# TensorE takes its work in a written-out order, and P is transposed by a product with identity columns, out of one pool of seven PSUM banks

## The chip, the core and the metric

The kernel runs on one core of a Trainium2 chip. Five engines matter: TensorE multiplies matrices and writes its results to PSUM (PE in the profile, with its weight loads as PEld), VectorE (DVE) and ScalarE (ACT) compute and copy, GpSimd (POOL) does small things, and SyncE (SP) issues DMAs. PSUM is taken by the kernel as eight banks of 128 partitions by 512 f32. The metric is device microseconds of one execution; less is better. The kernel before took 2958.28 us, the median of three runs (2955.21 to 2960.57).

## The reference

The input x has 2048 tokens of 576 numbers. Two layers follow one another, and each is a recurrent attention and a gated feed-forward part, with the same weights in both layers:

```python
x = x + _A_ref(_layernorm(x), mem0, Wq, Wk, Wv, Wo, 32)
x = x + _B_ref(_layernorm(x), w1, w3, w2)      # twice in all

def _A_ref(x, mem0, ...):                      # 32 heads of 128; 8 memory rows; 64 segments of 32 tokens
    for s in range(64):
        h = concatenate([mem, x[segment s]])   # 40 rows
        q, k, v = h @ Wq, h @ Wk, h @ Wv
        p = softmax(where(mask, q k^T * scale, -1e9))
        o = (p v) @ Wo
        mem = o[:8]                            # the next segment needs it
        outs.append(o[8:])

def _B_ref(x, ...):
    return (silu(x @ w1) * (x @ w3)) @ w2      # 4608 hidden numbers
```

The memory rows make the segments of one layer a chain: segment s+1 of a layer can't begin its products before the output product of segment s is through.

## The kernel before, in words

**Steps.** The work goes in 72 steps. Step t does segment t of the first layer and segment t - 8 of the second (`LAG` is 8). Steps 0 to 7 have the first layer alone and steps 64 to 71 the second alone, with 40 columns (32 tokens and 8 memory rows); steps 8 to 63 have both side by side, 80 columns, in the same instructions. The heads of a step go in four groups g of eight.

**Units of TensorE work.** `make_nodes` makes a list of nodes; each TensorE node is a run of matmuls that is never split. By one letter each, with the number of matmuls: Q (32, products of Wq and Wk with the segment, two per group) and q (8, the last 64 rows of that contraction); S (16, or 8 in a step of one layer: the scores of a group); T (8, the transposition of the softmax's result P of a group); P (16, P times V); O (40, the output product); X and x (32 and 8, V of the tokens), V and v (the same for the memory rows); F (36, the first products of the feed-forward part on one pair of hidden blocks; in the last job 16, with its remainder f as a unit of its own) and W (8, the second product); m, n, p (transpositions around layernorm and residual; 5 each; the list of the change has a, b and n for the three sorts that are all n here).

**Shapes of the array.** The units use the array in five ways, which the nodes carry as `mode`: full (128 rows by 128 columns of array: Q, T, O, W and the transpositions, and the first products F of the last job), row (64 rows: q, P, F, f), col (128 by 64: S), c32 (128 by 32: X, V) and oct (64 by 32: x, v).

**The order.** `plan` walks a model of the engines in time. At each step it takes the engine that can begin first, and for TensorE the waiting node with the best key: its priority, plus `o.wait` for a late start, plus a penalty `o.mode_pen` for a change of shape. The nodes of the other engines are taken by priority alone. A node marked AD goes to ScalarE or VectorE, whichever the model has free first. The list that comes out is emitted as it stands, and `ch` chains the instructions of each engine in that order, so the order is fixed when the kernel is built; on the chip each engine still waits for the data.

**PSUM.** Six banks form the pool `bank`; most units take two of them and give them back when VectorE or ScalarE has read them. The bank `YB` collects O over a step. The bank `SB` is a pool of one, `s`, and is used in turn by S (f32 scores, 320 columns) and T (bf16). The planner chooses the bank numbers.

**The softmax chain of a group.** S writes the scores; VectorE adds the mask, takes the maximum and subtracts it; ScalarE takes the exponential; VectorE sums, inverts and multiplies into the tile `PB`, which has the first layer's rows at 0 to 39 and the second's at 64 to 103, and zeros elsewhere where they matter. T (`ptr`) turns `PB` round with eight transposing matmuls against the first 104 columns of `ident`, and `pt_ev` copies the 40 or 80 wanted columns of each out of `SB` to `PTS` in one instruction. P reads `PTS`, `ot_ev` copies its two banks to `OT`, and O reads `OT`. After the last O of a step, `y_mem` copies the memory rows from `YB` into `HT`, which Q of the next step reads.

**In the profile** all matmuls stand under line L498, ScalarE's work under L501 and VectorE's under L504, so groups are told apart by their tiles: Q and q are `bank<-HT,W`, S is `SB<-QKT`, T is `SB<-ident,PB`, P is `bank<-PTS,VX` and `bank<-PTS,VM`, O is `YB<-OT,WO`, X, x, V, v are `bank<-WV,HT`, F is `bank<-XTB,W` and W is `bank<-W2C,HTT`.

Of the kernel before, what the change touches and what calls it, by code (L numbers as in the profile page):

```python
# [37 lines left out]
POOLS = {"bank": 6, "s": 1, "y": 1, "qkt": 4, "vx": 2, "vm": 1, "sme": 2, "pb0": 1, "pb1": 1, "pts": 1, "ot": 1,  # L38
# [29 lines left out]
def plan(nodes, pools, o):  # L68
# [12 lines left out]
    order = []  # L81

    def push(n):
        (both if n.eng == "AD" else ready[n.eng]).append(n)

    def slots_at(n):
        t = 0.0
# [3 lines left out]
        for p, c in need.items():  # L91
            f = sorted(free[p])
            t = max(t, f[c - 1])
# [5 lines left out]
    done = 0  # L99
    idle = 0.0  # L100
    while done < len(nodes):
        best = None
        for e in t_eng:
            cands = ready[e] + (both if e in ("ACT", "DVE") else [])
            if not cands:
                continue
            ests = [(max(t_eng[e], n.ready, slots_at(n)), n) for n in cands]
# [5 lines left out]
        if best is None:  # L113
            stuck = [(n.name, n.prio) for e in ready for n in ready[e]][:20]
            raise RuntimeError(f"the plan is stuck: {stuck}")
# [11 lines left out]
        st, n = min(pool_, key=key)  # L127
# [3 lines left out]
        if n.eng == "AD":  # L131
            both.remove(n)
        else:
            ready[e].remove(n)
        if e == "PE":
            idle += max(0.0, st - t_eng[e])
            if n.mode != mode:
                dur += SWITCH
                mode = n.mode
        n.start, n.end, n.by = st, st + dur, e  # L140
        t_eng[e] = n.end
        for s in n.acq:
            f = free[s.pool]
            ok = [i for i in range(len(f)) if f[i] <= st + 1e-9]
            s.i = min(ok, key=lambda i: f[i])
# [6 lines left out]
        for o_ in n.outs:  # L152
            lat = n.lat
# [979 lines left out]
```

## Time and profile before

| What | us |
|---|---|
| median of three runs | 2958.28 |
| the profiled execution, its own time | 2961.47 |
| its span, first to last instruction | 2959.4 |
| TensorE busy (matmuls) | 2870.1 |
| VectorE busy | 2060.5 |
| ScalarE busy | 1150.1 |
| TensorE's mean granted clock | 0.985 |

The profile is of one execution, so its own time is what its rows add up to, and the median is 3.2 us below it. A matmul's listed duration (about 200 ns for most) includes its way through the array and overlaps with the next one's; what a matmul costs TensorE is the distance from its start to the start of the next. So the costs are read from the starts of neighbouring rows in the timeline, not from the mean durations.

### The profile page before, as it was taken

What the parts mean: (1) busy time and instruction counts of PE and PEld (TensorE: products, weight loads), DVE (VectorE), ACT (ScalarE), POOL (GpSimd) and SP (SyncE); (2) the same over time, 40 slices, a digit from 0 to 9 for tenths busy, and PEclk for the clock granted to TensorE, in tenths of its full rate; (3) what the DMA queues carried; (4) which work ended last, traced back from release to release, by engine and by line L of the source; (5) the groups of instructions that cost most, each with busy time, mean ns of one, the idle gap of its engine ahead of it and who ended that gap; (6) DMA issues with size and microseconds to landing.
All of it is one profiled execution on the core that took longest, in us unless ns stands there. A gap on an engine that the chain in (4) does not pass through costs nothing.

```text
span 2959.4 us, 146757 instructions
## 1 busy us (share of the span) xinstructions
PE 2870.1 (97%) x67733; PEld 2328.3 (79%) x67733; DVE 2060.5 (70%) x4939; ACT 1150.1 (39%) x2759; POOL 63.6 (2%) x108
## 2 busy tenths in 40 slices
PE   5899999999999999999999999999999999999987
PEld 4777878788888878887887887888788888887876
DVE  3566676776777677676777777677767767776765
ACT  1334443343434343343434334343433434343332
POOL 0000000000000000000000000000000000000000
PEclk8899999999999999999999999999999999999998
DMA  9055544434443433444343443434344344434567
GB/s 299 4 117 125 114 106 109 109 88 108 99 99 93 109 101 93 105 100 106 91 100 96 109 100 90 115 91 107 89 109 108 87 109 97 99 94 114 125 152 221
DMA packets 483561, 324.43 MB, mean 110 GB/s; under 512 B 16888, under 2 KB 478080, under 8 KB 482944
## 3 DMA queue, kind: packets, MB, share of 16 engines
q1 hardware_dynamic: 479872, 307.96, 42.9%
q8 instruction: 529, 8.67, 1.3%
q0 software_dynamic: 3072, 7.08, 0.8%
q14 instruction: 88, 0.72, 0.1%
HBM read 310.26 MB, written 2.36 MB: 106 GB/s over the span
## 4 chain that ended last, share of the span: by engine, by line
PE 91%; DMA 3%; issue 2%; DVE 2%; ACT 1%; SPq 1%; POOL 0%; POOLq 0%; DVEq 0%; ACTq 0%
PE bank L498 71%; PE YB L498 12%; PE SB L498 7%; DMA W<-in_B_w_dram 1%; DMA W<-in_A_Wk_dram 1%; ACT HT L501 1%; SPq L507 1%; DVE SME L504 0%; DVE STAT L504 0%; DVE HTT L504 0%; DVE PB L504 0%; DMA W2C<-in_B_w_dram 0%; DVE XR L504 0%; DVE LNS L504 0%; ACT XTB L501 0%
## 5 line engine op out<-in xcount | busy, mean ns | idle before, releaser
L498 PEld LDWEIGHTS <-W 128*128 128x128 bf16 (+1 forms) x34256 | 1229.3, 97 | 138.0 <-issue 43.0
L498 PE MATMUL bank<-HT,W 128*128 128x80 bf16 (+2 forms) x23040 | 815.4, 197 | 8.9 <-issue 2.5
L498 PE MATMUL bank<-XTB,W 64*128 64x256 bf16 (+2 forms) x11216 | 619.6, 260 | 15.4 <-DMA W<-in_B_w_dram 9.7
L498 PE MATMUL bank<-WV,HT 128*32 128x512 bf16 (+3 forms) x8000 | 468.6, 387 | 12.2 <-DMA WV<-in_A_Wv_dram 5.7
L498 PE MATMUL YB<-OT,WO 128*128 128x80 bf16 (+1 forms) x11520 | 437.1, 198 | 8.9 <-ACT OT L501 2.9
L501 ACT ACTIVATE QKT<-bank 128x320 bf16<-128x320 f32 (+1 forms) x694 | 249.8, 405 | 487.4 <-PE bank L498 485.4
L498 PEld LDWEIGHTS <-WO 128*128 128x128 bf16 x11560 | 413.8, 99 | 30.2 <-issue 22.5
L498 PEld LDWEIGHTS <-HT 128*32 128x32 bf16 (+3 forms) x8000 | 174.4, 93 | 237.3 <-issue 99.2
L504 DVE TENSOR_REDUCE STAT<-SME 104x8 f32<-104x320 f32 (+1 forms) x576 | 277.2, 481 | 93.3 <-ACT SME L501 86.9
L504 DVE SCALAR_TENSOR_TENSOR HTT<-HTT,bank 128x512 bf16<-128x512 bf16 (+1 forms) x324 | 200.6, 619 | 202.1 <-ACT HTT L501 199.7
L504 DVE TENSOR_TENSOR PB<-SME,STAT 40x256 bf16<-40x256 f32 (+1 forms) x1024 | 320.9, 318 | 17.9
L504 DVE CAST QKT<-bank 128x320 bf16<-128x320 f32 (+1 forms) x458 | 198.7, 453 | 170.7 <-PE bank L498 170.2
L498 PE MATMUL bank<-W2C,HTT 128*128 128x288 bf16 x2232 | 315.2, 287 | 0.5
L501 ACT ACTIVATE HTT<-bank 128x512 bf16<-128x512 f32 (+1 forms) x324 | 177.7, 548 | 324.4 <-PE bank L498 323.1
L504 DVE SCALAR_TENSOR_TENSOR XR<-bank,XR 128x288 f32<-128x288 f32 x576 | 248.4, 453 | 75.0 <-PE bank L498 65.0
L498 PEld LDWEIGHTS <-HTT 128*128 128x128 bf16 x2304 | 208.4, 98 | 54.3 <-DVE HTT L504 2.6
L501 ACT ACTIVATE OT<-bank 128x320 bf16<-128x320 f32 (+1 forms) x394 | 149.5, 408 | 240.8 <-PE bank L498 240.2
L501 ACT ACTIVATE PTS<-SB 128x640 bf16<-128x640 bf16 (+1 forms) x250 | 162.2, 649 | 185.8 <-PE SB L498 185.3
L504 DVE TENSOR_TENSOR HTT<-HTT,bank 128x512 bf16<-128x512 bf16 (+1 forms) x324 | 203.6, 628 | 32.0 <-DVE HTT L504 0.5
L501 ACT ACTIVATE SME<-SME 104x320 f32<-104x320 f32 (+1 forms) x288 | 135.6, 471 | 209.8 <-DVE SME L504 209.0
L504 DVE CAST VX<-bank 128x512 bf16<-128x512 f32 x115 | 79.4, 691 | 136.4 <-PE bank L498 131.8
L504 DVE TENSOR_TENSOR SME<-SB,maskb 104x320 f32<-104x320 f32 (+1 forms) x288 | 140.5, 488 | 46.4 <-PE SB L498 42.0
(64 smaller groups left out, 1863.1 us busy)
## 6 DMA issues: line engine op xcount, KB each, us to landing
W<-in_B_w_dram SPq DMA_DIRECT2D x612, 288.0 KB, 4.7
W2C<-in_B_w_dram SPq DMA_DIRECT2D x306, 288.0 KB, 3.3
W<-in_B_w_dram SPq DMA_DIRECT2D x10, 512.0 KB, 9.8
XR<-in_A_x_dram POOLq DMA_DIRECT2D x16, 288.0 KB, 3.0
WO<-in_A_Wo_dram SPq DMA_DIRECT2D x4, 1152.0 KB, 9.0
W<-in_A_Wq_dram SPq DMA_DIRECT2D x8, 512.0 KB, 8.6
W<-in_A_Wk_dram SPq DMA_DIRECT2D x8, 512.0 KB, 9.7
WV<-in_A_Wv_dram SPq DMA_DIRECT2D x4, 1024.0 KB, 12.5
```

The costliest lines, as they stand in the source:

```text
L498: self.ch("PE", self.nc.tensor.matmul(out, lhsT=lhsT, rhs=rhs, start=start, stop=stop, skip_group_check=True, **k))
L501: self.ch("ACT", self.nc.scalar.activation(*a, **k))
L504: self.ch("DVE", getattr(self.nc.vector, fn_)(*a, **k))
L507: self.ch("SP", self.nc.sync.dma_start(out=out, in_=in_))
```

## The change

There are three edits. **The order:** `plan` takes a string `ORDER` with one letter per TensorE unit, and TensorE's next node is always the next letter's. The string is `FIRST` (707 letters), eleven times `FOUR` (194 letters, four steps), and `LAST` (590 letters); it has as many of each kind as before. ScalarE, VectorE, GpSimd and the DMAs are still placed by the model, by priority. **The transposition:** T becomes an ordinary product. `sel` holds 40 columns of the identity per layer (those at 0 and at 64), and each of T's eight matmuls multiplies `PB` with the 40 or 80 columns in use; the result is f32. T takes two banks of the pool, one for each half, and `pt_ev` becomes two copies, one per bank, each of 160 or 320 f32 columns, and each free to go to ScalarE or VectorE. **The pool:** `SB` is gone, the pool `bank` has seven banks, and S takes one of them.

```diff
-POOLS = {"bank": 6, "s": 1, "y": 1, "qkt": 4, "vx": 2, "vm": 1, "sme": 2, "pb0": 1, "pb1": 1, "pts": 1, "ot": 1,
+POOLS = {"bank": 7, "y": 1, "qkt": 4, "vx": 2, "vm": 1, "sme": 2, "pb0": 1, "pb1": 1, "pts": 1, "ot": 1,
...
+KINDS = {"m0tr": "m", "L0tr": "a", "L1tr": "b", "POST": "p", "Ftr": "n", "QK": "Q", "QKt": "q", "SC": "S", "TR": "T", "PV": "P",
+         "WO": "O", "VX": "X", "VXt": "x", "VM": "V", "VMt": "v", "FF": "F", "FFt": "f", "W2": "W"}
+def plan(nodes, pools, letters):
...
+    kinds = {}
+    for n in nodes:
+        if n.eng == "PE":
+            kinds.setdefault(KINDS[n.name], []).append(n)
+    its = {k: iter(v) for k, v in kinds.items()}
+    seq = [next(its[c]) for c in letters]
+    assert len(seq) == sum(len(v) for v in kinds.values())
...
+            if e == "PE":
+                cands = seq[at:at + 1] if at < len(seq) and seq[at].left == 0 else []
...
-        if e == "PE":
-            pool_ = [x for x in ests if x[0] <= t + o.hor]
-            work = {}
-            for x in pool_:
-                work[x[1].mode] = work.get(x[1].mode, 0.0) + x[1].dur
-            key = lambda x: (x[1].prio + o.wait * (x[0] - t)
-                             + (o.mode_pen - o.bulk * min(work[x[1].mode], 4.0) if x[1].mode != mode else 0.0))
-        else:
-            pool_ = [x for x in ests if x[0] <= t + 1e-9]
-            key = lambda x: x[1].prio
+        st, n = min((x for x in ests if x[0] <= t + 1e-9), key=lambda x: x[1].prio)
...
+FIRST = (
+    "maQQqqXVvxQSQXqQqSTqQPOTqPOSQxqTQqPSOTPXOxQQqqQqSQQqVSqvQTQqqQqPSTOSPOTPTOPaOQQqqQSqXQqQTSxQqqVvSQQqqPSTOPTOPTOP"
+    "OQQqqQQSqVqQSvQqqQTQqPqSXTOSPTOPOTxPXOxQpQqqVSQQqqnvQQSqqFTQQSqPqFOSTFPWTOPFTOPFOXxQQqqQQSqFqQWQSqqFVvSTQQqPqWTO"
+    "PSFOTFPTOWPFOaXxQQqqQQqSVqvQSqFQqWTQSPFqQqTOSPTOWPFTOPFOQQqqFVWQqSQvqFQQSqqFTQPqSWQOTqPSFTOPWTOPObVXxvQQqqpQSXqx"
+    "QnqQQTSqqQPSFqOQTqFPSFOTPFXxOTWPFOVvQqQQqqFSQQqqXxSQqWTQSPqFOTQqFPSTOWPFXTOxPFOWaQQqqQQSqqQVqSXvxQQqFqWTSQPFTOqP"
+    "FSOTFPXWTOxPFOFQQqQqQSqqQqXVvxQqSTSQPqWQOTqPFSOTWPFOTWPObppQXVqxnQqXxQqSQqnQqvQSqQTqFPFSTOQPqWOTSWPFOTXPFFxOWWQQ"
+    "qqQSqVXxvQQqqQSqTQSPqFOTQqFPSWTOFPWTOFPFXxWWOQQqqWSVXxvQaTQqqQQSqFqQQSqqFPWTOFPTWOSWPFXTOWPxXOWQqFxQQqFqSQqVQvSQ"
+    "qqQTWqSQWPqFTOPSTOPFOTWPWObVXxvpXxp"
+)
+FOUR = (
+    "QQqqnQnQSqqQQSqqFTQqFPSQTOqPFSOWTWFPFTOXPxWOWQQqqFSQQqqXVxvSWQTQqqFPSQQTOqqFPWTOaSPFXxOTWPFOWQQqqVvSWQQqqFTQQSqq"
+    "FPXSxOWTQQqqFFPSWTOWPFOTXxPFWOWQQqqVSvQQqqQQTSqqQQqPqSXxOTFPSWTOWPFTOWPWObVXxvppXx"
+)
+LAST = (
+    "QQqqQSnQqqQQqqSnTQPFqFSTOQPqFSOTWWPFXTOPFOxQQqqXxQQSqqWQSWQqqFFVSvTQqPQqTOPSTOFPXOxTWPWOFQQqqWWQQqqFSSQQqqVXxvWT"
+    "QqPSQTqOSFPWTOPFXTOxPWOWQQqFqQQqqFXSxQQSqqFTWQVvqQSqPWOTFPSFOTWWPFOTWPWObVvpQpQqqXxSQQqqnQnSqXxTQQqqQSqFPFTOSPTO"
+    "FPFTOPWOWQQqqVWWvSQQqFqQSqQTqQQqqSPFTOXPSxTOWPFOTFPWOFQqQqFSWWQqQQqFqVvSWTWQqFPFTWOQSqPQOWqFTSFPXWFxTOWPFOWQQqqQ"
+    "SQqqVSvQQqqTQSPqQqTOSPWOTFPTOWPOWpbVXvxnQQqqQQSqFqQQSqqXQTxSqQPqFTOSPWTOFPFTOPWOXxFQQqqQSqFVvQTqFSQWQqqFPSQQFqqO"
+    "TWPSTOPFOTFPXOFxQWQqqQQSqqQqVSFvQTqQPqFSWQqTOSPFTOPFOTWPOQQqqQQSqVvqFQTqSQqPQSqQqWTSOPOTFPTOPOpnWFfFfFfFWFfFfWfF"
+    "fFWfFFWffFfFfWFfFWFffFfWFfFfWW"
+)
+ORDER = FIRST + FOUR * 11 + LAST
...
-            s = Slot("s")
+            s = banks(1)[0]
...
-            pt = Slot("s")
             pts = Slot("pts")
-            tr = node("PE", 8 * 0.046, em.ptr(t, g, pb, pt), deps=[pbs], prio=pf + o.tr, mode="full", acq=[pt, pts], rel=[pb], name="TR")
-            pe_ = node("AD", ewh(8 * c80), em.pt_ev(t, g, pt, pts), deps=[tr], prio=pf, rel=[pt], name="PTe")
+            bt = banks()
+            tr = node("PE", 8 * mm80, em.ptr(t, g, pb, bt), deps=[pbs], prio=pf + o.tr, mode="full", acq=[pts] + bt, rel=[pb], name="TR")
+            pe_ = [node("AD", ew(4 * c80), em.pt_ev(t, g, m, bt[m], pts), deps=[tr], prio=pf, rel=[bt[m]], name="PTe") for m in (0, 1)]
             b = banks()
             ot = Slot("ot")
-            pv = node("PE", 8 * mm80, em.pv(t, g, pts, vx_slots[t, k], b), deps=[pe_] + vme + vx_nodes[t, k], prio=pf + o.pv,
+            pv = node("PE", 8 * mm80, em.pv(t, g, pts, vx_slots[t, k], b), deps=pe_ + vme + vx_nodes[t, k], prio=pf + o.pv,
...
-    def ptr(self, t, g, pb, pt):
-        def f(n):
-            PT = self.T.SB[:].bitcast(BF)[:, 0:GH * 104].rearrange("p (h q) -> p h q", h=GH)
-            for m in (0, 1):
+    def ptr(self, t, g, pb, b):
+
+        def f(n):
+            q0, q1 = self.qcols(t)
+            nq = q1 - q0
+            for m, T in enumerate(self.bk(x) for x in b):
                 for hl in range(4):
-                    self.mm(PT[:, 4 * m + hl, :], self.T.PB[0:104, g % 2, m, 2 * hl:2 * hl + 2, :], self.T.ident[0:104, 0:104],
-                            True, True, is_transpose=True)
-        return f
-
-    def pt_ev(self, t, g, pt, pts):
-        def f(n):
-            ls = self.layers(t)
-            nq = QW * len(ls)
-            b = self.T.SB[:].bitcast(BF)[:, 64 * ls[0]:64 * ls[0] + 1]
-            src = bass.AP(b.tensor, b.offset, [list(b.ap[0]), [104, GH], [64, len(ls)], [1, QW]])
-            dst = self.T.PTS[:, pts.i, 0:GH * nq].rearrange("p (h a q) -> p h a q", h=GH, a=len(ls))
-            self.cp(n, dst, src)
+                    self.mm(T[:, hl * nq:(hl + 1) * nq], self.T.PB[0:104, g % 2, m, 2 * hl:2 * hl + 2, :], self.T.sel[0:104, q0:q1],
+                            True, True)
+        return f
+
+    def pt_ev(self, t, g, m, b, pts):
+        def f(n):
+            q0, q1 = self.qcols(t)
+            w = 4 * (q1 - q0)
+            self.cp(n, self.T.PTS[:, pts.i, m * w:(m + 1) * w], self.bk(b)[:, 0:w])
         return f
...
+    T.sel = sp.tile([P, 2 * QW], BF, name="sel")
-    T.SB = pp.tile([P, 512], F32, name="SB")
+    for li in (0, 1):
+        nc.gpsimd.tensor_copy(T.sel[:, li * QW:(li + 1) * QW], T.ident[:, R64 * li:R64 * li + QW])
-    nc.vector.memset(T.SB[:], 0.0)
-    order, _ = plan(nodes, pools, Opt)
-    for n in order:
+    for n in plan(nodes, pools, ORDER):
```

More of the change, by code (lines that the diff above doesn't have):

```diff
@@ L143, in plan @@
             f = free[s.pool]
-            ok = [i for i in range(len(f)) if f[i] <= st + 1e-9]
-            s.i = min(ok, key=lambda i: f[i])
+            s.i = min((i for i in range(len(f)) if f[i] <= st + 1e-9), key=lambda i: f[i])
             f[s.i] = NOW
@@ L151, in plan @@
                 free[s.pool][s.i] = s.end
-        for o_ in n.outs:
-            lat = n.lat
-            if o_.eng == e == "PE":
-                lat = 0.0
-            o_.ready = max(o_.ready, n.end + lat)
-            o_.left -= 1
-            if o_.left == 0:
-                push(o_)
+        for m in n.outs:
+            m.ready = max(m.ready, n.end + (0.0 if m.eng == e == "PE" else n.lat))
+            m.left -= 1
+            if m.left == 0:
+                push(m)
         order.append(n)
-        done += 1
-    return order, idle
+    return order
 def actc(*ns):
```

41 lines of the change are left out of this document (19 added, 22 removed).

## The prediction

> **What bounds the kernel now.** I read the page first: the engines' totals and the chain that ended last.
>
> ```profile
> span 2959.4 us, 146757 instructions
> PE 2870.1 (97%) x67733; PEld 2328.3 (79%) x67733; DVE 2060.5 (70%) x4939; ACT 1150.1 (39%) x2759; POOL 63.6 (2%) x108
> ...
> PE 91%; DMA 3%; issue 2%; DVE 2%; ACT 1%; SPq 1%; POOL 0%; POOLq 0%; DVEq 0%; ACTq 0%
> ```
>
> TensorE is busy 97% of the span and is 91% of the chain. Since an average hides stages, the next view is the busy time by stretches (first column the stretch, then its length and each engine's busy time, granted clock, DMA share).
>
> ```profile
> core 0: us, PE busy (x) PEld busy (x) DVE busy (x) ACT busy (x) POOL busy (x), PEclk, DMA share, GB/s
> 0.00:278.00 278.00, 229.48 (x6392) 181.10 (x6393) 150.12 (x414) 88.92 (x275) 8.67 (x21) 0.91 0.54 141
> ...
> 448.00:2660.00 2212.00, 2207.40 (x50214) 1788.53 (x50213) 1598.44 (x3752) 889.95 (x2029) 48.35 (x76) 1.00 0.42 100
> 2660.00:2960.00 300.00, 267.97 (x6752) 219.55 (x6750) 191.25 (x467) 95.71 (x274) 3.44 (x6) 0.93 0.61 153
> ```
>
> TensorE's waits in the long middle stretch, all that are listed for it (total us, times, longest):
>
> ```profile
> PE bank L498 <- ACT HT L501: 3.0, 5, 0.6
> ...
> PE bank L498 <- ACT XTB L501: 0.6, 1, 0.6
> ...
> PE bank L498 <- issue: 0.5, 1, 0.5
> ```
>
> In the middle TensorE idles 4.6 us of 2212 (2212.00 - 2207.40): it waits for nothing. So there the time is the sum of what the matmuls cost in TensorE's own line, and only two things can shorten it: cheaper units and cheaper neighbours. Waits are left in the first 278 us (48.5 idle) and the last 300 (32.0 idle).
>
> What a unit costs is read from the starts in the timeline of TensorE (start, length with the pipeline's end, then the group):
>
> ```profile
> 1424.06 0.54 PE L498 MATMUL SB<-ident,PB 104*128 104x104 bf16 x8
> 1424.43 1.60 PE L498 MATMUL YB<-OT,WO 128*128 128x80 bf16 x40
> 1425.96 0.43 PE L498 MATMUL SB<-QKT 128*64 128x40 bf16 x16
> ...
> 1426.72 1.15 PE L498 MATMUL bank<-W2C,HTT 128*128 128x288 bf16 x8
> 1427.71 1.60 PE L498 MATMUL YB<-OT,WO 128*128 128x80 bf16 x40
> 1429.14 0.54 PE L498 MATMUL SB<-ident,PB 104*128 104x104 bf16 x8
> 1429.51 1.15 PE L498 MATMUL bank<-W2C,HTT 128*128 128x288 bf16 x8
> 1430.59 0.21 PE L498 MATMUL bank<-PTS,VX 64*128 64x80 bf16 x2
> ...
> 1436.24 1.60 PE L498 MATMUL YB<-OT,WO 128*128 128x80 bf16 x40
> ```
>
> and, a period later,
>
> ```profile
> 1606.13 1.60 PE L498 MATMUL YB<-OT,WO 128*128 128x80 bf16 x40
> ```
>
> W costs 0.99 when O follows in the same array shape (1426.72 to 1427.71) and 1.08 when P follows in another (1429.51 to 1430.59). O costs 1.43 before T in the same shape (1427.71 to 1429.14) and 1.53 before S (1424.43 to 1425.96). So a change of shape costs 0.09 to 0.10 us, and I take 0.095. The two rows at 1436.24 and 1606.13 are each the last O of a step, four steps apart: a period of the middle is 1606.13 - 1436.24 = 169.9 us.
>
> **Part 1, the order: fewer changes of shape.** Written as letters, the TensorE rows of that period have 194 units and 119 changes of shape. `FOUR` has the same 194 units, so the same matmuls, and by its letters 90 changes (the last letter to the first included). That is 29 fewer in each of eleven periods, 319. Over the whole, from m to the last W, the rows have 2090 changes and the string has 1759; 331 fewer x 0.095 = **31.4 us** less. Nothing hides this, since TensorE waits for nothing there, and nothing is added to it: the same work stands closer.
>
> **Part 2, T with fewer columns.** T is 8 matmuls of 104 columns in 0.37 us (1424.06 to 1424.43), 46 ns each. The new one has 80 columns in two-layer steps; a matmul of that size, with weights of 128 columns, is O: 1.43 / 40 = 36 ns, so T becomes 0.286 us. In steps of one layer the new T has 40 columns:
>
> ```profile
> 2860.11 0.53 PE L498 MATMUL SB<-ident,PB 104*128 104x104 bf16 x8
> 2860.47 0.96 PE L498 MATMUL bank<-HT,W 128*128 128x40 bf16 x32
> ...
> 2880.34 0.97 PE L498 MATMUL bank<-HT,W 128*128 128x40 bf16 x32
> 2881.15 1.14 PE L498 MATMUL bank<-W2C,HTT 128*128 128x288 bf16 x8
> ```
>
> There T costs 0.36 and a matmul of 40 columns 0.81 / 32 = 25 ns, so T becomes 0.20. The groups of instructions by shape (count, busy us, mean ns) have the counts, in the mask addition, one per group of heads; the weight loads of O and T; and the copies of T's result and, for their new size, of P's; and the feed-forward's work between F and W (HTT):
>
> ```profile
> L498 PEld LDWEIGHTS <-WO 128*128 128x128 bf16 x11552 | 413.6, 99 | 29.8 <-issue 22.3 <-DMA WO<-in_A_Wo_dram 2.9
> ...
> L504 DVE TENSOR_TENSOR HTT<-HTT,bank 128x512 bf16<-128x512 bf16 x252 | 173.3, 688 | 24.9 <-DVE HTT L504 0.5
> ...
> L501 ACT ACTIVATE HTT<-bank 128x512 bf16<-128x512 f32 x252 | 150.0, 595 | 253.4 <-PE bank L498 252.2
> ...
> L501 ACT ACTIVATE PTS<-SB 128x640 bf16<-128x640 bf16 x197 | 138.9, 705 | 140.1 <-PE SB L498 139.9
> L501 ACT ACTIVATE OT<-bank 128x320 bf16<-128x320 f32 x312 | 126.8, 436 | 196.6 <-PE bank L498 196.6
> ...
> L498 PEld LDWEIGHTS <-PB 104*128 104x128 bf16 x2304 | 117.9, 99 | 59.9 <-issue 19.6 <-DVE XR L504 7.8 <-DVE PB L504 7.7
> ...
> L504 DVE TENSOR_TENSOR SME<-SB,maskb 104x320 f32<-104x320 f32 x224 | 109.4, 488 | 26.7 <-PE SB L498 23.4
> ...
> L504 DVE CAST OT<-bank 128x320 bf16<-128x320 f32 x136 | 65.7, 483 | 0.4
> ...
> L504 DVE TENSOR_TENSOR SME<-SB,maskb 40x320 f32<-40x320 f32 x64 | 31.1, 487 | 19.7 <-PE SB L498 18.6
> ...
> L504 DVE COPY PTS<-SB 128x640 bf16<-128x640 bf16 x27 | 13.3, 492 | 10.6 <-PE SB L498 9.4 <-ACT HTT L501 1.1
> ```
>
> 224 x 0.084 = **18.8 us**, and 64 x 0.16 = 10.2 us at most; the 64 lie in the first and last stretches, where TensorE is busy 86% of the time ((229.48 + 267.97) / 578), so I take **8 us**. No row of before has an f32 product against identity columns, so its price has two ends: 36 ns as O, and the old 46 ns, which gives nothing. I take the first: the weight loads of T and of O both take 99 ns and lie under other matmuls, and 104 columns at 46 ns and 80 at 36 are the same 0.45 ns a column.
>
> The Trainium skill, page "TensorE: Matmul & The Clock Gate", section "Back-to-back issue gap", says that in a real stream of weight loads and matmuls both set the spacing, and gives about 81 ns for 128 columns. By that, fewer columns under the same weight load would save nothing, and this part would give 0 instead of 27 us. The trace disagrees: O, with 128-column weights, runs at 36 ns.
>
> **Part 3, the copies and the banks.** One copy of 640 bf16 (705 ns on ScalarE, 492 on VectorE) becomes two of 320 f32 (436 or 483 each). Both on one engine, they take 0.87 to 0.97 us; one on each, 0.48. The work added is at most 2 x 483 - 492 = 474 ns a T, 16 x 0.474 = 7.6 us in a period of about 166, on a VectorE that is at 72% (1598.44 / 2212): to 79%. So no engine but TensorE becomes the bound; what can appear is lateness. Between T and its P the period has at the least one W with its change, 1.08 us, once (T W P), and more than 1.6 us at the other fifteen. After T the copy needs this:
>
> ```profile
> 1424.69 0.70 ACT L501 ACTIVATE PTS<-SB 128x640 bf16<-128x640 bf16 x1
> ```
>
> The copy starts 0.26 us after TensorE has moved on (1424.43), so two copies on one engine are through after 0.26 + 0.97 = 1.23 at the latest, if that engine is free. The one short place lacks 0.15 us; the others have 0.4 us and more to spare. The same goes for the memory rows: `FOUR` has O W Q at three of its four step ends, where Q needs the first of these copies.
>
> ```profile
> 1437.87 0.62 ACT L501 ACTIVATE HT<-YB 128x64 bf16<-128x64 f32 x3 [2.03 <-PE YB L498]
> ```
>
> All three end at 1437.87 + 0.62, 0.82 us after O at 1437.67 (1436.24 + 1.43), and W covers 0.99. If ScalarE is in the middle of a copy of 0.44 then, the first of the three is still in time.
>
> The banks are what the trace can't tell. S no longer has to wait for T's copy out of `SB`, which can give back at most the idle 4.6 us; T takes two of seven banks instead of one of its own, and whoever wants a pair may find it late. A bank missing until a copy ends costs up to 0.48 us, at each of 16 T in 14 periods 108 us. Between a gain of 4.6 and a loss of 108 I take **3 us of loss**: the period of before runs without waits on six banks and one, and the seven are the same number. If the cover is gone, the next thing late is O behind P, then Q behind O.
>
> **Part 4, first and last stretches.** Their 80.5 us of idle time (48.5 + 32.0) are many kinds of wait; the longest of the first stretch, as listed, are these:
>
> ```profile
> PE SB L498 <- DVE PB L504: 5.8, 4, 3.3
> PE bank L498 <- DMA WV<-in_A_Wv_dram: 5.7, 2, 3.2
> PE bank L498 <- DVE bank L1093: 4.8, 1, 4.8
> PE bank L498 <- DVE XN L504: 4.6, 1, 4.6
> ```
>
> The set-up (L1093), the first weights and the first layernorm (XN) are there in any order; the softmax's chain (PB) is the sort that an order can cover better or worse. I take 0, between a gain of a quarter of the idle time, 20 us, and a loss of 15, as if a quarter of T's in these stretches (16 of 64) waited 0.9 us more, two copies in a row. The set-up has one memset fewer for `SB` and one more for the seventh bank, and two small copies on GpSimd, which has 98% to spare: 0.
>
> **The sum.** From the profiled execution's 2961.5: 2961.5 - 31.4 - 18.8 - 8 + 3 = 2906.3. The median of the runs is 3.2 below the profiled one, so **2903 us**, 1.9% less.
>
> **The rivals.** *The ends gain too.* The quarter of the idle 80.5 us is covered by other work, 20 us: 2903 - 20 = **2883**. For it: the two ends have their own letters and need not follow a rule made for the middle; against: the chains of one layer stay as long.
>
> *T gets no cheaper.* If the weight load or the f32 result paces it, the 27 us of part 2 are gone: 2903 + 27 = **2930**. For it, nothing in the rows beyond that this kind of product is not among them; against it, the 36 ns of O. The page's rule above is this rival.
>
> *TensorE waits for copies or banks, and the kernel is slower.* Place: T to P and the pair of banks before T in the middle. T's two copies stand in the queues of ScalarE and VectorE behind a tanh or a product of the feed-forward part (0.60 and 0.69 us a piece) and P waits; O is queued behind P. It decides from 58 / 288 = 0.20 us per T on, where all the gain is eaten. With 0.35 us per T, 288 x 0.35 = 101 us, it is 2903 - 3 + 101 = **3001**. For it: VectorE would go to 79%, and T needs two banks at once. Against: T W P, the shortest cover, stands 48 times in the order of before, where T's one copy needs up to 0.26 + 0.70 = 0.96 us, and yet TensorE waits only 4.6 us in the middle; `FOUR` has it once.
>
> **How the numbers follow.** The main case 0.62, with its own range 2893 to 2918; the ends gain 0.15; T no cheaper 0.09; waits 0.14, of which 0.06 end below 2952, 0.03 between 2952 and 2964, and 0.05 above. A measurement of this kernel tells about 0.2%, 6 us, from nothing. Faster: 0.62 + 0.15 + 0.09 + 0.06 = 0.92; within 0.2%: 0.03; slower: 0.05. The range 2878 to 2932 takes in the ends and a T no cheaper, and leaves out most of the waits.
>
> **What would show it.** A period of four steps should take 169.9 - 29 x 0.095 - 16 x 0.084 = 165.8 us; W to P still 1.08 and W to O 0.99; T 0.29 from start to start; TensorE's idle time in the middle stretch below 10 us. The prediction is wrong if T stays at 0.37, if a change of shape costs other than 0.095, or if TensorE's waits for PTS, OT or banks in the middle come to tens of us.

## The result, and the profile after

The changed kernel takes 2889.84 us (median of four runs, 2887.82 to 2894.47), 2958.35 us for the kernel before on the same chip: a ratio of 0.9771, with a 95% interval of 0.9754 to 0.9788, or 68 us less. The prediction was 2903 us with a range of 2878 to 2932, so the measured time is inside the range and 13 us below the main figure. The profiled execution took 2887.82 us.

The page of the changed kernel, its totals and the shares of the chain that ended last:

```profile
span 2885.8 us, 147090 instructions
PE 2801.2 (97%) x67733; PEld 2302.7 (80%) x67733; DVE 2077.1 (72%) x5053; ACT 1139.2 (39%) x2933; POOL 63.1 (2%) x110
...
PE 83%; issue 6%; DVE 5%; DMA 4%; ACT 1%; SPq 1%; POOL 0%; POOLq 0%; DVEq 0%; ACTq 0%
```

TensorE runs as many matmuls as before and is busy 68.9 us less (2870.1 - 2801.2). Its share of the chain fell from 91 to 83%, the rest going to VectorE and to "issue". The same stretches as before, with the ends moved along with the kernel (columns as before: stretch, length, busy time of each engine, granted clock):

```profile
core 0: us, PE busy (x) PEld busy (x) DVE busy (x) ACT busy (x) POOL busy (x), PEclk, DMA share, GB/s
0.00:278.00 278.00, 232.17 (x6757) 186.67 (x6759) 162.73 (x456) 93.77 (x300) 8.87 (x23) 0.92 0.53 141
448.00:2600.00 2152.00, 2144.29 (x49971) 1766.00 (x49971) 1595.82 (x3796) 879.66 (x2165) 47.73 (x76) 1.00 0.43 102
2600.00:2886.00 286.00, 259.27 (x6763) 212.98 (x6757) 193.94 (x486) 94.72 (x286) 3.38 (x6) 0.97 0.62 161
```

The middle still waits for almost nothing: 7.7 us of 2152, where before had 4.6 of 2212. The longest of TensorE's waits there (total us, times, longest):

```profile
PE bank L519 <- DVE HTT L525: 2.2, 10, 0.2
PE bank L519 <- DMA W2C<-in_B_w_dram: 1.8, 2, 1.5
```

TensorE's timeline in a period of the middle (start, length, group; the lines are now L519, L522 for ScalarE and L525 for VectorE, and T is `bank<-sel,PB`):

```profile
1405.57 1.60 PE L519 MATMUL YB<-OT,WO 128*128 128x80 bf16 x40
...
1431.83 0.46 PE L519 MATMUL bank<-sel,PB 104*128 104x80 bf16 x8
1432.12 1.60 PE L519 MATMUL YB<-OT,WO 128*128 128x80 bf16 x40
1433.65 0.32 PE L519 MATMUL bank<-HT,W 64*128 64x80 bf16 x8
...
1437.95 1.15 PE L519 MATMUL bank<-W2C,HTT 128*128 128x288 bf16 x8
1438.93 0.45 PE L519 MATMUL bank<-sel,PB 104*128 104x80 bf16 x8
1439.22 1.15 PE L519 MATMUL bank<-W2C,HTT 128*128 128x288 bf16 x8
1440.30 0.94 PE L519 MATMUL bank<-XTB,W 64*128 64x256 bf16 x14
...
1571.54 1.60 PE L519 MATMUL YB<-OT,WO 128*128 128x80 bf16 x40
```

The first and the last row are each the last O of a step, four steps apart: a period is 165.97 us. T takes 0.29 us to the next unit's start (1431.83 to 1432.12, 1438.93 to 1439.22). W takes 0.98 into T, of its own shape, and 1.08 into F, of another (1439.22 to 1440.30); O takes 1.53 into q, of another shape (1432.12 to 1433.65).

Cut at the last O of every fourth step, the two profiles differ like this:

| Stretch | before, us | after, us | difference |
|---|---|---|---|
| steps 0 to 15 | 586.6 | 576.1 | -10.5 |
| steps 16 to 59, eleven periods | 1872.3 | 1827.8 | -44.5 |
| steps 60 to 71 and the last feed-forward part | 500.5 | 481.9 | -18.6 |

So the middle gives 4.0 us a period. Each column is one execution: the two profiles lie 73.6 us apart, the medians 68.5, and about 5 us of the table belong to these two executions. The eleven periods repeat to 0.2 us in the two profiles that there are of the changed kernel, so the 5 us most likely lie in the ends: by the medians the ends give some 24 us, about a third of the gain.

### The profile page after: what moved, and what is told of

Same layout as the page of the kernel before. It is cut to its first block, busy times and chain, and to the rows that moved or that the text cites. A ratio compares the mean times of both kernels' runs of the same rounds, so it can differ in the third digit from the quotient of the medians.

```text
span 2885.8 us, 147090 instructions
## 1 busy us (share of the span) xinstructions
PE 2801.2 (97%) x67733; PEld 2302.7 (80%) x67733; DVE 2077.1 (72%) x5053; ACT 1139.2 (39%) x2933; POOL 63.1 (2%) x110
## 4 chain that ended last, share of the span: by engine, by line
PE 83%; issue 6%; DVE 5%; DMA 4%; ACT 1%; SPq 1%; POOL 0%; POOLq 0%; DVEq 0%; ACTq 0%
PE bank L519 72%; PE YB L519 10%; DMA W<-in_B_w_dram 2%; DMA W<-in_A_Wk_dram 1%; DVE XR L525 1%; DVE HTT L525 1%; DVE STAT L525 1%; SPq L528 1%; DVE LNS L525 1%; DVE PB L525 1%; DVE SME L525 1%; DMA W2C<-in_B_w_dram 1%; DVE OT L525 0%; DVE XN L525 0%; ACT SME L522 0%
## 5 line engine op out<-in xcount | busy, mean ns | idle before, releaser
L519 PEld LDWEIGHTS <-W 128*128 128x128 bf16 (+1 forms) x34256 | 1231.1, 97 | 124.2 <-issue 34.3
L519 PE MATMUL bank<-HT,W 128*128 128x80 bf16 (+2 forms) x23040 | 805.9, 197 | 13.3 <-ACT HT L522 3.9
L519 PE MATMUL bank<-XTB,W 64*128 64x256 bf16 (+1 forms) x11216 | 616.6, 259 | 6.3 <-DMA W<-in_B_w_dram 4.6
L519 PE MATMUL bank<-WV,HT 128*32 128x512 bf16 (+3 forms) x8000 | 451.6, 384 | 11.3 <-DMA WV<-in_A_Wv_dram 10.1
L519 PE MATMUL YB<-OT,WO 128*128 128x80 bf16 (+1 forms) x11520 | 437.9, 198 | 14.2 <-issue 7.0
L522 ACT ACTIVATE QKT<-bank 128x320 bf16<-128x320 f32 (+1 forms) x773 | 272.9, 409 | 434.1 <-PE bank L519 430.8
L519 PEld LDWEIGHTS <-WO 128*128 128x128 bf16 x11560 | 412.3, 99 | 37.6 <-issue 31.3
L519 PEld LDWEIGHTS <-HT 128*32 128x32 bf16 (+3 forms) x8000 | 172.4, 93 | 219.0 <-issue 68.0
L525 DVE TENSOR_TENSOR PB<-SME,STAT 40x256 bf16<-40x256 f32 (+1 forms) x1024 | 320.5, 318 | 16.6
L519 PE MATMUL bank<-W2C,HTT 128*128 128x288 bf16 x2232 | 324.9, 288 | 5.6 <-DVE HTT L525 2.5
L525 DVE TENSOR_REDUCE STAT<-SME 104x8 f32<-104x320 f32 (+1 forms) x576 | 276.4, 480 | 67.7 <-ACT SME L522 59.9
L522 ACT ACTIVATE HTT<-bank 128x512 bf16<-128x512 f32 (+1 forms) x324 | 177.8, 549 | 341.7 <-PE bank L519 341.6
L525 DVE SCALAR_TENSOR_TENSOR HTT<-HTT,bank 128x512 bf16<-128x512 bf16 (+1 forms) x324 | 201.6, 622 | 107.8 <-ACT HTT L522 103.3
L525 DVE SCALAR_TENSOR_TENSOR XR<-bank,XR 128x288 f32<-128x288 f32 x576 | 245.1, 448 | 32.6 <-PE bank L519 27.8
L525 DVE CAST QKT<-bank 128x320 bf16<-128x320 f32 (+1 forms) x379 | 159.2, 443 | 137.8 <-PE bank L519 135.8
L519 PEld LDWEIGHTS <-HTT 128*128 128x128 bf16 x2304 | 205.0, 98 | 66.7 <-issue 10.5
L522 ACT ACTIVATE PTS<-bank 128x320 bf16<-128x320 f32 (+1 forms) x389 | 146.1, 404 | 197.8 <-PE bank L519 189.9
L525 DVE TENSOR_TENSOR HTT<-HTT,bank 128x512 bf16<-128x512 bf16 (+1 forms) x324 | 203.4, 628 | 23.3 <-DVE HTT L525 1.8
L522 ACT ACTIVATE SME<-SME 104x320 f32<-104x320 f32 (+1 forms) x288 | 135.0, 469 | 192.5 <-DVE SME L525 188.9
L525 DVE TENSOR_TENSOR SME<-bank,maskb 104x320 f32<-104x320 f32 (+1 forms) x288 | 140.1, 487 | 89.1 <-PE bank L519 84.5
L522 ACT ACTIVATE OT<-bank 128x320 bf16<-128x320 f32 (+1 forms) x346 | 133.2, 404 | 162.6 <-PE bank L519 155.9
L522 ACT ACTIVATE VX<-bank 128x512 bf16<-128x512 f32 x166 | 95.1, 596 | 179.7 <-PE bank L519 179.5
```

The source lines that it names most:

```text
L519: self.ch("PE", self.nc.tensor.matmul(out, lhsT=lhsT, rhs=rhs, start=start, stop=stop, skip_group_check=True, **k))
L522: self.ch("ACT", self.nc.scalar.activation(*a, **k))
L525: self.ch("DVE", getattr(self.nc.vector, fn_)(*a, **k))
```

## The experiments

Every kernel below computes the whole function. Ratios are to the kernel before in runs on the same chip, with 95% intervals; the gain or loss between two kernels is the difference of their ratios times 2958 us; with these intervals such a difference is known to 4 to 9 us. A period is the mean of the eleven (steps 16 to 59 of the profiled execution), 170.2 us before and 166.2 in the changed kernel, except where two rows are shown for it. Single periods differ: the pair of rows in the prediction, 169.9, is one of the short ones of before, and the 165.97 above one of the short ones after.

### Which of the three edits gives it

**New T and pool, order of before.** The string is the order in which the kernel before ran, as letters (2090 changes of shape).

```diff
-ORDER = FIRST + FOUR * 11 + LAST
+ORDER = (
+    ...
```

> The changed kernel (T as a product, seven banks), with the 3431 TensorE units in the order of the kernel before. Theory A, the parts add up: T and the pool alone give 18.8 + 8 us, so 2958 - 27 = 2931 us (2924 to 2940), T 0.29 us from start to start, a period of four steps 169.9 - 16 x 0.084 = 168.6 us with 119 changes of shape. Theory B, the new T only pays with an order made for it (two banks a T, two copies): TensorE waits for banks or copies of T in the middle, a period above 169.5, the whole above 2945.

Measured: 2928.13 us, ratio 0.9906 (0.9886 to 0.9926), period 168.8. The two edits without the order give what was expected of them together, to 3 us. What each of the two gave is taken apart below, and there it is not as expected.

**Written order, T and banks of before.** `SB` is back with S and T in turn, beside six banks, and T's matmuls and its one copy are those of before.

```diff
-POOLS = {"bank": 7, "y": 1, ...
+POOLS = {"bank": 6, "s": 1, "y": 1, ...
...
-            s = banks(1)[0]
+            s = Slot("s")
...
-            bt = banks()
-            tr = node("PE", 8 * mm80, em.ptr(t, g, pb, bt), ...
+            pt = Slot("s")
+            tr = node("PE", 8 * 0.046, em.ptr(t, g, pb, pt), ...
```

> The kernel before (transposing T of 104 columns, the bank SB shared by S and T, six banks in the pool) with the written-out order. Theory A, the parts add up: 331 fewer changes of shape x 0.095 = 31 us, a period of 169.9 - 2.8 = 167.1 us, the whole about 2927 us (2915 to 2935). Theory B, the order needs the pool of seven: where it sets S close to T, or more pairs of banks close together, than SB and six banks allow, TensorE waits for SB or a bank, tens of us in the middle, a period of 168.5 or more, the whole above 2940.

Measured: 2975.69 us, ratio 1.0065 (1.0050 to 1.0080), period 171.3. The order that was to save 31 us costs 19 us by itself. The first expectation is missed by 49 us, and the second one's side is right, but the kernel is even slower than before. The waits of TensorE over the whole of this kernel say why:

```profile
PE SB L517 <- DVE SME L523: 41.5, 47, 1.6
PE SB L517 <- ACT PTS L520: 14.4, 19, 0.9
```

T waits for `SB` until the mask addition has read the scores out of it (SME), and S until T's copy has (PTS): 56 us, for one bank. One of them in the timeline of all engines:

```profile
1469.98 1.32 PE L517 MATMUL bank<-HT,W 128*128 128x80 bf16 x32
...
1470.77 0.69 DVE L523 SCALAR_TENSOR_TENSOR HTT<-HTT,bank 128x512 bf16<-128x512 bf16 x1
...
1471.49 0.69 DVE L523 TENSOR_TENSOR HTT<-HTT,bank 128x512 bf16<-128x512 bf16 x1
1472.10 0.48 DVE L523 TENSOR_TENSOR SME<-SB,maskb 104x320 f32<-104x320 f32 x1
...
1472.63 0.53 PE L517 MATMUL SB<-ident,PB 104*128 104x104 bf16 x8 [1.33 <-DVE SME L523]
```

At 1469.98 TensorE went on from S to one Q, and behind it stood T. The mask addition stood behind a copy to `OT` and two products of the feed-forward part in VectorE's queue until 1472.10, and TensorE stood still for 1.33 us until the bank was read. The letters had this in them: in the order of before at least two units lie between S and the next T, at all 132 places of the eleven periods, and at least one between T and the next S. `FOUR` has one unit between S and T at three of its twelve places, and none between T and S at one.

**Seven shared banks, T of before, both orders.** T is transposing again, in bf16, with 104 columns, one bank and one copy, but its bank and that of S come from the pool of seven. First with the written order:

```diff
-            bt = banks()
-            tr = node("PE", 8 * mm80, em.ptr(t, g, pb, bt), ..., acq=[pts] + bt, ...
-            pe_ = [node("AD", ew(4 * c80), em.pt_ev(t, g, m, bt[m], pts), ...) for m in (0, 1)]
+            bt = banks(1)[0]
+            tr = node("PE", 8 * 0.046, em.ptr(t, g, pb, bt), ..., acq=[pts, bt], ...
+            pe_ = [node("AD", ewh(8 * c80), em.pt_ev(t, g, bt, pts), ...)]
...
-                    self.mm(T[:, hl * nq:(hl + 1) * nq], self.T.PB[...], self.T.sel[0:104, q0:q1], True, True)
+                    self.mm(PT[:, 4 * m + hl, :], self.T.PB[...], self.T.ident[0:104, 0:104], True, True, is_transpose=True)
```

> The changed kernel with T as it was before (transposing, 104 columns, bf16, one bank, one copy of 640), but out of the pool of seven, as S; the written-out order. It differs from the written-out order on the old banks only in where S and T write. Theory A, the single bank SB shared by S and T was what made the written-out order slow there: a period of 166.1 + 1.2 = 167.3 us, the whole 2900 to 2912 us, like the 104-column product. Theory B, T's one long copy (0.70 us on ScalarE), late for P, was it: a period above 169 us and the whole above 2930 us.

Measured: 2905.36 us, ratio 0.9831 (0.9805 to 0.9857), period 167.2, as the first theory had it. Against the kernel with `SB`, the same T and the same order take 69 us less, with nothing changed but where the banks come from (and how the planner then places the work of the other engines). And with the order of before:

```diff
-ORDER = FIRST + FOUR * 11 + LAST
+ORDER = (
+    ...
```

> This kernel has the order of before and the transposed P of before (bf16, 104 columns, one bank, one copy); only the pool changes: seven banks, of which the scores and the transposed P take one each, where before had six and one bank of their own. The order of before waited for nothing in the middle (4.6 us idle of 2212), so theory A says that the pool by itself gives that order nothing: 2955 us (2948 to 2960), a period of 170.2 us, and the 27 us between before and the kernel with the old order, new T and seven banks are all the price of T's columns. Theory B says that the shared pool lets some copies come earlier in the first and last stretches too, where TensorE does wait: 2940 us (2930 to 2948), all of the gain in the first 16 steps and the last 12.

Measured: 2951.24 us, ratio 0.9976 (0.9966 to 0.9987), period 169.9. That is within the range of the first theory, but the pool is not worth nothing: 7 us, of which 3.5 (0.32 x 11) lie in the eleven periods. To the written order it is worth 69.

**Six banks for everything.**

```diff
-POOLS = {"bank": 7,
+POOLS = {"bank": 6,
```

> The changed kernel with six banks in the pool instead of seven (the eighth is left empty); the order and T as they are. Theory A, the written-out order needs the seventh bank, as its slowness on the old banks says: TensorE waits for banks in the middle, a period above 168.5 us, the whole above 2920 us. Theory B, seven is more than it needs: a period below 167 us, the whole 2885 to 2900 us.

Measured: 2964.16 us, ratio 1.0034 (1.0024 to 1.0044), period 170.9: 78 us more than with seven, and slower than before. The stretch from 600 to 2380 us, and TensorE's waits in it:

```profile
600.00:2380.00 1780.00, 1752.04 (x40286) 1443.36 (x40282) 1292.85 (x3064) 713.26 (x1751) 39.95 (x63) 1.00 0.42 100
```

```profile
PE bank L519 <- DVE HTT L525: 7.7, 19, 0.5
PE bank L519 <- ACT QKT L522: 5.0, 20, 0.3
PE bank L519 <- ACT PTS L522: 4.4, 10, 0.4
```

28.0 us idle in 1780, where the kernel with seven has 4.3 in the same stretch, spread over many short waits for whichever copy or product frees a bank. That is 2.3 us a period ((28.0 - 4.3) / 10.4), and the period is 4.7 longer. The other half is late starts that are not listed as idle: a matmul's listed 0.2 us runs on past the point where the next could have started, so a delay shorter than that counts as busy. In the next rows T takes 0.45 us to the next unit's start, not 0.29, with no idle time marked; in the trace its fifth matmul, the first into its second bank, starts 0.18 us after the fourth.

```profile
1438.14 0.62 PE L519 MATMUL bank<-sel,PB 104*128 104x80 bf16 x8
1438.59 1.60 PE L519 MATMUL YB<-OT,WO 128*128 128x80 bf16 x40
```

The seven cases side by side:

| T | banks | order | us | ratio | period, us |
|---|---|---|---|---|---|
| 104 columns | six and `SB` | before | 2958.3 | 1 | 170.2 |
| 104 columns | six and `SB` | written | 2975.69 | 1.0065 | 171.3 |
| 104 columns | seven shared | before | 2951.24 | 0.9976 | 169.9 |
| 104 columns | seven shared | written | 2905.36 | 0.9831 | 167.2 |
| 80 columns | seven shared | before | 2928.13 | 0.9906 | 168.8 |
| 80 columns | seven shared | written | 2889.84 | 0.9771 | 166.2 |
| 80 columns | six shared | written | 2964.16 | 1.0034 | 170.9 |

### What T's form costs

**The f32 product with all 104 columns.**

```diff
-                    self.mm(T[:, hl * nq:(hl + 1) * nq], self.T.PB[...], self.T.sel[0:104, q0:q1], True, True)
+                    self.mm(T[:, hl * 104:(hl + 1) * 104], self.T.PB[...], self.T.ident[0:104, 0:104], True, True)
```

(The copies then take their 40 or 80 columns out of each 104.)

> The changed kernel, but T multiplies by all 104 columns of the identity (f32, the same banks, the same two copies, which pick the 40 or 80 wanted columns of each 104). Theory A, a matmul's columns set its price: T back at 0.37 us from start to start, a period of 166.0 + 16 x 0.084 = 167.3 us, the whole 2890 + 18.8 + 8 = 2917 us (2910 to 2922). Theory B, the transposing form or its bf16 result made the old T dear: T stays near 0.29, the whole within 5 us of 2890.

Measured: 2906.51 us, ratio 0.9836 (0.9816 to 0.9855), period 167.3. The price is the first theory's, the time is below its range. In this kernel's timeline T is back at 0.37 us, as the transposing one was:

```profile
1438.62 0.53 PE L519 MATMUL bank<-ident,PB 104*128 104x104 bf16 x8
1438.99 1.60 PE L519 MATMUL YB<-OT,WO 128*128 128x80 bf16 x40
```

So the number of columns sets T's price, and an f32 result costs TensorE no more than a transposition. This kernel, with two banks and two copies per T, and the one above with one bank and one copy agree within their intervals: the form of the copies is worth nothing that shows. The columns are worth 19 us by this kernel and 18 by the one above, where 27 were expected. The price of the smaller T isn't what falls short: in a step of one layer the changed kernel's T, with 40 columns, takes 0.21 us to the next unit's start, where the prediction had 0.20 and before had 0.36.

```profile
2700.01 0.37 PE L519 MATMUL bank<-sel,PB 104*128 104x40 bf16 x8
2700.22 1.16 PE L519 MATMUL YB<-OT,WO 128*128 128x40 bf16 x40
```

**Both of T's copies on VectorE.**

```diff
-            pe_ = [node("AD", ew(4 * c80), em.pt_ev(t, g, m, bt[m], pts), ...
+            pe_ = [node("DVE", dve(4 * c80), em.pt_ev(t, g, m, bt[m], pts), ...
```

> The changed kernel with both copies of each T on VectorE, so that they follow one another (2 x 0.48 us) on the busier engine. Theory A, the order covers T's copies, as the distances from T to P say: at most 8 us more, 2886 to 2898 us. Theory B, VectorE's lateness reaches TensorE (the softmax chain or P waits): 0.2 us or more per T, 58 us, above 2930 us.

Measured: 2921.39 us, ratio 0.9884 (0.9860 to 0.9907), between the two expectations: 33 us more. 12 us of it (1.1 x 11) are in the eleven periods (167.2 each), the rest in the ends. What TensorE waits for in the middle is mostly not these copies but the softmax's result, which stands in the same queue:

```profile
PE bank L519 <- DVE PB L525: 9.3, 29, 0.6
PE bank L519 <- DVE XN L525: 2.4, 11, 0.2
```

VectorE is busy 75% of that kernel's span and 78% of its middle (1384.51 of 1780). In the changed kernel the planner shares the copies out, two thirds of those of 320 columns to ScalarE:

```profile
L522 ACT ACTIVATE PTS<-bank 128x320 bf16<-128x320 f32 x298 | 121.7, 435 | 172.0 <-PE bank L519 166.1 <-issue 2.0 <-DVE HTT L525 1.5
...
L525 DVE CAST PTS<-bank 128x320 bf16<-128x320 f32 x150 | 71.7, 478 | 31.5 <-PE bank L519 29.8 <-ACT PTS L522 1.4
```

### What a change of shape costs

Eight times in the period QQqq becomes QqQq: the same units, two changes of shape more each time, 106 instead of 90.

```diff
-FOUR: QQqqnQnQSqqQQSqqFTQq...
+FOUR: QqQqnQnQSqqQQSqqFTQq...
```

> The changed kernel with the eight places QQqq of the period turned into QqQq: the same units, 16 more changes of shape in each of the eleven periods, 106 instead of 90. Theory A, a change of shape costs 0.095 us wherever it stands: a period of 166.1 + 16 x 0.095 = 167.6 us, the whole 2890 + 16.7 = 2907 us (2902 to 2911). Theory B, the changes of shape are not what the order saved (it is how the waits fall): within 4 us of 2890.

Measured: 2910.07 us, ratio 0.9844 (0.9816 to 0.9872). Two rows of this kernel, the last O of steps four apart:

```profile
1415.69 1.60 PE L519 MATMUL YB<-OT,WO 128*128 128x80 bf16 x40
...
1583.35 1.60 PE L519 MATMUL YB<-OT,WO 128*128 128x80 bf16 x40
```

The period is 167.66 us, 1.69 more than the 165.97 of the changed kernel for 16 changes: 0.106 us each. TensorE idles no more in the middle than in the changed kernel (4.0 us of 1780 against 4.3), so the time went into the changes.

### The order of the first and the last steps

**Written order in the eleven periods alone.** The first 707 and the last 590 letters are those of before; `FOUR` and everything else stay. That makes 12 changes of shape more, 1.2 us.

```diff
-FIRST = ("maQQqqXVvxQSQXqQqSTqQPOTqPOSQxqT...
+FIRST = ("maQqQqSTXVQqvxXPQqxSOTQqPQqSOTPQ...
...
-LAST = (...
+LAST = (...
```

> The changed kernel with the written-out order in its eleven periods alone; the first 707 and the last 590 units stand in the order of the kernel before. This is for the 15 us that the ends gave beyond the sum of T's columns and the changes of shape. Theory A, the order of the ends gave it, by fewer waits and so less time at half clock in the last steps: about 2890 + 12 x 0.095 + 14 = 2905 us (2899 to 2912), and the last eight steps (last O of step 63 to last O of step 71) about 12 us longer than the 267.4 of the changed kernel. Theory B, T's shorter chain and the seventh bank gave it: 2891 us (2886 to 2896).

Measured: 2908.52 us, ratio 0.9835 (0.9821 to 0.9850), 19 us more. Steps 64 to 67 and 68 to 71, in the changed kernel:

```profile
2572.20:2711.30 139.10, 137.14 (x3568) 111.97 (x3565) 106.56 (x256) 50.84 (x153) 1.71 (x3) 1.00 0.52 119
2711.30:2839.60 128.30, 114.96 (x3491) 95.05 (x3488) 84.75 (x223) 49.33 (x155) 1.71 (x3) 0.97 0.65 170
```

and with the ends of before:

```profile
2583.50:2724.80 141.30, 138.13 (x3573) 112.76 (x3570) 104.58 (x253) 54.77 (x160) 2.53 (x4) 1.00 0.48 116
2724.80:2861.50 136.70, 120.01 (x3504) 98.58 (x3500) 87.15 (x229) 48.84 (x153) 2.29 (x4) 0.93 0.66 170
```

In the last four steps 8.4 us are lost: 5.05 in TensorE's busy time, at a lower granted clock (0.93 for 0.97), and 3.35 in idle time. Over the whole, the two profiles are 21.6 us apart: 7.4 in steps 0 to 15, 4.2 in steps 60 to 63, 2.2 and 8.4 in the two stretches shown, and next to nothing elsewhere.

Such figures for an end come from one execution each, and they vary. This kernel and the one with new T and pool in the order of before run the same instructions on every engine in steps 0 to 15, on the same chip. The last O of step 15 begins at 575.88 us in that kernel (its matmuls stand under L551) and at 582.15 in this one, 6.3 us later:

```profile
575.88 1.60 PE L551 MATMUL YB<-OT,WO 128*128 128x80 bf16 x40
```

```profile
582.15 1.60 PE L519 MATMUL YB<-OT,WO 128*128 128x80 bf16 x40
```

That kernel also gives a second estimate of what the order of the ends is worth. The written order saves 40 us against it (0.9906 to 0.9771), of which 29 lie in the eleven periods, so 11 are left for the ends, where this kernel says 19. Both are known to some 7 us only.

**Two other orders, with fewer changes of shape in the ends.** All three strings are replaced by ones found by exchanging neighbours; the period keeps its 90 changes. The changed kernel ran again beside them. The cut shows the first of the two.

```diff
-FIRST = ("maQQqqXVvxQSQXqQqSTqQPOTqPOSQxqT...
+FIRST = ("maQXxQVqqQSvqQTPOQqSXQqTqSPQqxTOQ...
...
-LAST = (...
+LAST = (...
```

> The changed kernel as it is, for comparison with the two orders beside it: 2890 us (2886 to 2895).

> The changed kernel with another written order: the units of the first steps, of the period and of the last steps are exchanged with neighbours so that there are fewer changes of the array's shape in the two ends (first 425 to 408, last 344 to 316; the period keeps 90) and no more than one unit stands between the ones that depend on one another where it did before. Theory A (the price of a change adds up as it did in the period, 0.10 us each, if the ends wait no more): 45 fewer are 4.5 us, so 2885.5 us (2881 to 2888). Theory B (in the ends the waits set the time, and a change of shape there lies in a wait): 2890 us (2886 to 2895), with the gain in busy time given back as idle time of TensorE. If the new neighbours uncover softmax or copy chains, it is above 2895.

> As the order beside it, another one: changes of shape in the first steps 425 to 396, in the last 344 to 329, the period keeps 90; 44 fewer. Theory A: 44 x 0.10 = 4.4 us less, 2885.6 us (2881 to 2888). Theory B: 2890 us (2886 to 2895). Above 2895 if the new neighbours uncover waits.

Measured: the changed kernel 2890.46 us, ratio 0.9769 (0.9756 to 0.9782); the first order 2891.92 us, 0.9769 (0.9755 to 0.9782); the second 2900.98 us, 0.9806 (0.9792 to 0.9819). The 45 changes saved in the ends of the first order show nothing in the time, though with intervals of 4 us each way a gain of 4.5 us is near the limit of what can be told. The second is 10.5 us slower with 44 fewer, and that is clear. The first order's profile (its fastest execution, 2885.53 us), from 2600 us to its end at 2883.5, against the 286 us above:

```profile
2600.00:2960.00 360.00, 254.51 (x6605) 210.22 (x6600) 188.17 (x472) 92.15 (x284) 3.38 (x6) 0.96 0.49 126
```

TensorE has 29.0 us idle there (2883.5 - 2600 leaves 283.5 of the span, less 254.51), against 26.5 (285.8 less 259.27). So in this end some waits were added, as the second theory has it; that they eat the whole gain is not shown. Which unit's place decides in the ends was not found, and no order better than the given one either.

## Why the prediction was right, and where it was wrong

**What bounds it, and the price of a change of shape: right.** 0.095 us were read from neighbouring rows and 0.106 measured by adding changes. With the seven shared banks the written order takes 2.7 us off a period with the old T (169.9 to 167.2) and 2.6 with the new one (168.8 to 166.2), and 29 x 0.095 was 2.76.

**The period: right, 165.97 against 165.8.** Its parts are a little other than foretold: order 2.7 (2.76), T's columns 1.0 to 1.1 (1.34; 167.2 to 166.2 and 169.9 to 168.8), and the pool, which was down as a loss, gains 0.3. Of what T's columns lack in the written order, 0.2 is idle time: the changed kernel idles 4.3 us in 1780 of its middle, the one with 104 columns and one bank 2.3.

**T: right in its price, its worth mis-sized.** 0.286 us were expected and 0.29 is in the rows, and the rival in which T gets no cheaper is out: its price goes by columns whatever the kind of product. The 27 us of the two terms are 18 to 19 in the written order (the two kernels with 104 columns) and 21 in the order of before (0.9976 to 0.9906), each known to 7 to 9 us. In the eleven periods, where the figure is firm, they are 1.1 x 11 = 12 of the 14.8 that 176 T's were to give; the rest of the gap lies in the ends, where the price of the smaller T was right too (0.21 for 0.20) and the runs don't say what took the gain back.

**The order's term: the step that failed is that "nothing hides this, since TensorE waits for nothing there, and nothing is added to it", with Part 3's "the seven are the same number".** The cover was read from a trace whose own order had been made with one bank for S and T: at least two units from S to T. `FOUR` puts them closer, which the written letters show without any run, and on `SB` its waits (56 us) cost more than its 31 us are worth. So the three edits are no sum: the pool alone gives 7 us, the order alone loses 19, the two together give 50 (0.9831), and T another 18. With the pool there, the order's term was too small, not too large: it is worth 43 us (50 less 7) for the 31.4 of the sum, 30 of them in the periods as forecast and the rest in the ends. The prediction charged 3 us for the pool and bounded its gain by 4.6, the idle time of an order that didn't need it. The total came out well because all three edits are there together, and in part by luck: T gave 9 us less than its term, the pool 10 more and the order 12 more. The rival with waits for banks named a real risk: with one bank fewer 78 us are lost, where it had 101, though the waits then stand at many units and not at T alone.

**The copies: the working held for what the planner does, and not beyond.** With either engine to choose from, TensorE idles 7.7 us in the whole middle, below the 10 that were allowed. The price of losing that choice is 33 us, at a VectorE 78% busy in the middle; Part 3 counted 79% there as harmless because no engine but TensorE would be the bound, and what went late was the softmax's last product, in the same queue.

**The ends: mis-sized.** Part 4 took 0 between a gain of 20 us and a loss of 15. By the two profiles the ends gave 29.1 us (10.5 + 18.6), by the medians 24, of which the terms had about 13: T's 8, 48 T's of two layers outside the periods at 0.084 (4.0), and 12 changes of shape (1.1). That leaves 11 to 16. The order of the ends is worth 11 us by one pair of kernels and 19 by another, 1.2 of it for 12 changes of shape, so it can account for what is left, within intervals of some 7 us. So 2889.84 lies between the main case (2903) and the rival in which the ends gain too (2883), nearer to the rival. That the gain there comes with less idle time and a higher granted clock is shown by the two profiles; which neighbours bring it is not.

## What to carry to other kernels

A stage in which nothing waits tells what its own order hides, not what another order will need: before an order is charged for its matmuls alone, walk the new one for each single buffer and count the units between who fills it and who needs it empty. Edits that tie together (an order, a buffer pool, the engine that frees a buffer) are costed as one case and tested at the corners, since the worth of one may change its sign with the other. Where TensorE never waits, a price read from the starts of neighbouring rows, per change of shape and per column, held here to about a tenth. Where it does wait, the starts are also the better measure: with six banks half of the lost time was not listed as idle.

## What the runs showed of the hardware

**A lower granted clock at the ends, and its price.** The first two rows below are O's of one layer in the timeline of the kernel before, the second of them the last O of step 71; in the next fence the row at 2838.65 is that same last O in the changed kernel (in brackets the idle time before, and what ended it):

```profile
2872.78 1.17 PE L498 MATMUL YB<-OT,WO 128*128 128x40 bf16 x40
...
2912.05 1.49 PE L498 MATMUL YB<-OT,WO 128*128 128x40 bf16 x40 [0.43 <-ACT OT L501]
```

```profile
2827.61 0.37 PE L519 MATMUL YB<-OT,WO 128*128 128x40 bf16 x8
2830.35 0.97 PE L519 MATMUL YB<-OT,WO 128*128 128x40 bf16 x32 [2.38 <-issue]
...
2838.65 1.16 PE L519 MATMUL YB<-OT,WO 128*128 128x40 bf16 x40 [0.39 <-ACT OT L522]
```

The same 40 matmuls take 1.17 or 1.49 us. The trace lists the granted clock in stretches: before has 0.5 for 23.9 us from 2900.2 on, with the row of 1.49 in it, and the changed kernel 6.8 us from 2843.1 on. In these two profiles all such stretches lie in the first and last 300 us, where TensorE has most of its idle gaps too. In the kernel with 106 changes of shape in a period two more lie further in, of 3.4 us each, from 359.8 and 523.7 us on, right behind gaps of 1.21 us (to 359.3) and 2.29 us (to 523.7). The changed kernel has gaps of 1.15 and 1.52 us at the same places and keeps the full clock there. So a gap of over a microsecond does not always bring a lower clock with it; whether gaps bring it on at all was not tried.

**Stops inside a run of matmuls.** The row at 2830.35 is the rest of an O of 40 that stood still for 2.38 us after its eighth matmul, with nothing that the profile shows to wait for ("issue"). Over the whole of the changed kernel:

```profile
PE bank L519 <- issue: 13.7, 18, 2.2
...
PE YB L519 <- issue: 7.0, 8, 2.4
```

20.7 us, all but 0.6 of it outside the middle; before had 13.0, 2.9 and 2.4 more for `SB`. They lie in the stretches in which the DMA share is high (0.53 and 0.62 in the first and last rows of the stretches above, 0.43 in the middle). Within single stops it is not always so: it is 0.95 from 2828.0 to 2830.3, and 0.03 in a stop of 1.38 us that ends at 202.3. What causes them no run here tells.
